# A soft-cap attention with a soft mixture of experts on one core: who takes four exponential tiles, and the order of the first and last stages

## The chip, the cores and the metric

The kernel runs on one NeuronCore of one Trainium2 chip. The metric is the device time of one execution in microseconds (us), the median over several runs. The engines are PE (matrix multiply; PEld are its weight loads), DVE (vector), ACT (activations), POOL and SP; SP, POOL and ACT also issue DMA transfers.

## The reference

```python
# q, k, v: 8 batches x 12 heads x 448 x 64; cap = 30; 8 experts, 4 slots each
scores = cap * tanh((q @ k.T / sqrt(64)) / cap)
attn = softmax(scores)                 # over the 448 keys
x = (attn @ v), heads joined           # 3584 x 768
logits = x @ phi                       # 3584 x 32
d = softmax(logits, axis=0); c = softmax(logits, axis=1)
slot_input = d.T @ x                   # 32 x 768, 4 rows per expert
slot_out[e] = relu(slot_input[e] @ w1[e]) @ w2[e]     # 768 -> 1024 -> 768
out = c @ slot_out                     # 3584 x 768, float32
```

The softmax over the rows of `logits` runs over all 3584 tokens.

## The kernel before

**Attention.** Two heads of four make a pair, and a pair's scores are seven tiles of 128 x 448. There are 48 pairs, so 336 tiles, laid in one order and cut into `NCH` = 56 chunks of six. A chunk j takes two score groups from PE (three tiles each, into one of two PSUM buffers `sc`), two tanh on ACT (L301, 1344 columns each) that write the tile `ex` of the chunk, and an exponential over the chunk in place (L305, `exp_chunk`), which is issued one chunk later. Five `ex` buffers rotate.

**Shared tiles.** In most chunks ACT's exponential leaves out the first tile (`exp_part(j, len(shared[j]), CH)`, 2240 columns in place of 2688). DVE computes that tile with five operations, numbered 0 to 4 in `poly_exp` (L332 to L337), on one scratch tile `work`. `PARTS` tells, for each j modulo 7 save 4, in which slot of which chunk each operation stands, and `EXTRA` does the same for chunks 3, 4, 5 and 50 to 53.

**Order of work.** The order is written out by hand: each chunk has slots ("a", "b", "c", "d" and some more), `at(j, slot, f)` puts a job into one, and `run(j, slot)` issues its jobs, those marked "<" first and those marked ">" last. Each engine works through its own instructions in that order and waits on semaphores for the others. Matmuls with V (`pv`, L355), the division by the row sum (L362, L365), transposes, logits, exponentials of logits and slot sums follow two chunks and more behind. `spare`, `fill` and `busy` issue matmuls on ones whose results nobody reads.

**Head.** `first_pieces` brings the first two heads into place: casts to bf16 on DVE and ACT, transposes on PE ("turn", L219) into PSUM tiles, copies back (L221). It works in two parts of q (tiles 0 to 3, 4 to 6) and of k (0 to 2, 3 to 6). The first score group (L292) needs all of q and the first part of k.

**End of attention.** After the last chunk (j = 55) its exponential is issued in three parts. Pairs 46 and 47 are multiplied in halves (`pvm`, `pvl`), then come the last logits, their exponential `E`, the last slot sums, and `e_norm`, which adds up the sums of `E` in `zacc` and, in the last batch, gives `rz`, the reciprocal that scales both experts' first layer. `clear_hpad` clears a padded tile for the hidden activations on POOL; it lies where `work` lay. `id32` is an identity in float32 for the last logits.

**Experts and output.** `layer1(i, half)` (L747) gives 512 of 1024 hidden columns of four experts at a time; `relu` reads them from PSUM; `h_transp` puts them into `hpad`. `layer2` (L780) goes through 64 blocks for the first 384 output columns, `so[0]` takes the result, then again for the other 384, `so[1]`. The output has 28 tiles of 128 x 768 (64 rows from each of two batches): `half_tile` makes one half of one tile with a matmul (L815), a multiply on ACT or DVE (L819, L817) and a store of 192 KB (`obh`). The first halves of the first ten tiles are put between the blocks of the second `layer2`; those of tiles 10 and 11 come after the copy of `so[1]`. Then the second halves of the first `NH` tiles follow, and the remaining tiles are made whole (L862, L869, L871) and stored two at a time (`ob`, 768 KB). SP issues every store (L796), and before that the loads of the second layer's weights, `w2t` (L729).

Of the kernel before, what the change touches and what calls it, by code (L numbers as in the profile page):

```python
# [10 lines left out]
BF16 = mybir.dt.bfloat16  # L11
I32 = mybir.dt.int32
U16 = mybir.dt.uint16
ALU = mybir.AluOpType
ACT = mybir.ActivationFunctionType
PSUM = bass.MemoryType.PSUM

P = 128
HP = 64
NT = 7  # L20
DH = 64
S = 448
CH = 6
CS = 3
# [12 lines left out]
def kernel(  # L37
# [12 lines left out]
    B, H, _, _ = q.shape  # L50
# [5 lines left out]
    HD = D // 2  # L56
    NFT = F // P
    cap = float(cap)
# [4 lines left out]
    NPAIR = 2 * NQ  # L63
# [145 lines left out]
    def first_pieces(h, jobs):  # L209

        for stage, nm, c0, c1, eng, bank, at0 in jobs:
            copy = act.copy if eng is act else dve.tensor_copy
            cols = slice(h * HP, h * HP + HP)
            if stage == "cast":
                copy(casts[nm, 0][:, c0:c1, cols],
                     raws[nm, 0][h][:, c0 * DH:c1 * DH].rearrange("p (c d) -> p c d", d=DH))
            elif stage == "turn":
                for c in range(c0, c1):
                    pe.transpose(bank[cols, at0 + c - c0, :], casts[nm, 0][:, c, cols], ident)  # L219
            else:  # L220
                copy(qkT[nm, 0][cols, c0:c1, :], bank[cols, at0:at0 + c1 - c0, :])  # L221

    def first_half(h):
        for nm in ("k", "q"):
            if h == 0:
                qkT[nm, 0] = qk.tile([P, NT, P], BF16, name=nm + "T", tag=nm + "T")
        one = psT.tile([P, 8, P], BF16, name="ps1", tag="T")
        two = psV.tile([P, NT, P], BF16, name="ps2", tag="pv")
        if h == 0:

            three = boots[1][:, CS - 1, :].bitcast(BF16).rearrange("p (c q) -> p c q", q=P)
            first_pieces(h, (("cast", "q", 4, NT, act, None, 0), ("cast", "k", 0, CS, dve, None, 0),
                             ("cast", "q", 0, 4, dve, None, 0), ("turn", "q", 4, NT, pe, three, 0),
                             ("turn", "k", 0, CS, pe, two, 0), ("copy", "q", 4, NT, act, three, 0),
                             ("turn", "q", 0, 4, pe, one, 0), ("copy", "k", 0, CS, dve, two, 0),
                             ("cast", "k", CS, NT, act, None, 0), ("copy", "q", 0, 4, dve, one, 0),
                             ("turn", "k", CS, NT, pe, three, 3), ("copy", "k", CS, NT, dve, three, 3)))
        else:
            first_pieces(h, (("cast", "k", 0, NT, dve, None, 0), ("cast", "q", 0, NT, dve, None, 0),
                             ("turn", "k", 0, NT, pe, two, 0), ("turn", "q", 0, NT, pe, one, 0),  # L240
                             ("copy", "k", 0, NT, dve, two, 0), ("copy", "q", 0, NT, dve, one, 0)))
            for nm in ("q", "k"):
                raws.pop((nm, 0)), casts.pop((nm, 0))
                load(nm, 2)
# [59 lines left out]
    def exp_part(j, u0, u1):  # L304
        act.activation(exs[j][:, u0:u1, :], exs[j][:, u0:u1, :], ACT.Exp, scale=cap)  # L305

    def exp_chunk(j):
        exp_part(j, len(shared.get(j, ())), CH)

# [8 lines left out]
    EXTRA = {3: (((0, "a", (0,)), (0, ">b", (1,)), (0, "<d", (2, 3)), (1, "a", (4,)),),), 4: (((0, "a", (0,)), (0, ">d", (1, 2)), (1, "<b", (3,)), (1, "r", (4,)),),), 5: (((0, ">b", (0,)), (0, "<d", (1,)), (0, ">d", (2, 3)), (1, "r", (4,)),),), 50: (((0, "<d", (0,)), (0, ">d", (1, 2, 3)), (1, "a", (4,)),),), 51: (((0, "<b", (0,)), (0, ">b", (1,)), (0, ">d", (2,)), (1, ">b", (3, 4)),),), 52: (((0, "c", (0, 1)), (0, "<d", (2,)), (0, ">d", (3, 4)),),), 53: (((0, "<b", (0,)), (1, "a", (1,)), (1, "<b", (2,)), (1, "<d", (3,)), (1, ">d", (4,)),),)}  # L318
    shared = {j: (PARTS[j % 7],) for j in range(6, NCH - 6) if j % 7 in PARTS}
    shared.update(EXTRA)  # L320
    if cap >= 50:
        shared = {}

    lead = POW2[0] / FRAC ** 3
    p2, p1, p0 = (c / POW2[0] * FRAC ** (n + 1) for n, c in enumerate(POW2[1:]))
    halves16 = xe.bitcast(U16).rearrange("p (s two) -> p s two", two=2)
    frac, whole = halves16[:, :, 0], halves16[:, :, 1]

    def poly_exp(j, u, ops):
        t = exs[j][:, u, :]  # L330
        steps = (
            lambda: dve.tensor_scalar(xe, t, cap * math.log2(math.e) * FRAC,  # L332
                                      (127 + math.log2(lead)) * FRAC, ALU.mult, ALU.add),
            lambda: dve.tensor_scalar(xb.bitcast(U16), whole, 7, None, ALU.logical_shift_left),  # L334
            lambda: dve.scalar_tensor_tensor(xp, frac, p2, frac, ALU.add, ALU.mult),  # L335
            lambda: dve.scalar_tensor_tensor(xp, xp, p1, frac, ALU.add, ALU.mult),  # L336
            lambda: dve.scalar_tensor_tensor(t, xp, p0, xb, ALU.add, ALU.mult))  # L337
        for n in ops:
            steps[n]()
# [175 lines left out]
    def at(j, slot, f, *a):  # L515
        if j < 0:
            j, slot = 0, "b"
        aux.setdefault((j, slot), []).append((f, a))

    def clear_hpad():  # L520

        hpads.append(consts.tile([P, E, NFT, NS], BF16, name="hpad", tag="work", bufs=1))
        pool.memset(hpads[0], 0.0)
# [19 lines left out]
    for b in range(B):  # L543
# [20 lines left out]
        if b < B - 1:  # L564
# [6 lines left out]
                at(*when("en"), e_norm, b)  # L571
            if b % 2:
                at(*when("es"), e_sums, b // 2)
    for j, tiles in shared.items():
        for u, parts in enumerate(tiles):
            for dj, slot, ops in parts:
                at(j + dj, slot, poly_exp, j, u, ops)
    for n, job in enumerate(wjobs):
        at(1 + n * (NCH - 5) // len(wjobs), "b", *job)
    for j, slot, n in ((0, "a", 10), (0, "c", 10), (1, "b", 10), (1, "c", 8)):  # L580
        at(j, slot, spare, n)
    for j, slot, n in ((NCH - 6, "d", 8), (NCH - 4, "d", 8), (NCH - 2, "d", 12)):
        at(j, slot, spare, n)
    at(0, "c", init_vbd, 0)
    at(1, "c", init_vbd, 1)
    at(0, "d", vcast, 0)

    def run(j, slot):
        for part in ("<", "", ">"):
            for f, a in aux.pop((j, part + slot), []):  # L590
                f(*a)
# [6 lines left out]
    def busy(n, home=None, by=None):  # L598
        by = ones if by is None else by
        for _ in range(n):  # L600
            pe.matmul(junk if home is None else home, by, by, start=True, stop=True)  # L601
# [13 lines left out]
    for j in range(NCH):  # L615
# [31 lines left out]
        run(j, "c")  # L647
        qk_chunk(2 * j + 3)
        run(j, "d")
    last = NPAIR - 1  # L650
    assert place[last, 0] == NTILE - NT and pair_at[NCH - 3] == last - 2
    CL = CS
    exp_part(NCH - 1, len(shared.get(NCH - 1, ())), CL)
    exp_part(NCH - 1, CL, CH - 1)
    exp_part(NCH - 1, CH - 1, CH)
    attp.close()
# [3 lines left out]
    def bank(shape, dt=F32, name="bank"):  # L660
        return big.tile(shape, dt, name=name, tag="b")
# [5 lines left out]
    pv2 = [bank([P, 4, W], name=f"pvl{half}") for half in range(2)]  # L667
    junk = bank([P, P], name="junk")
    xq_tile(last - 1)
    run(NCH - 1, "t0")  # L670
    for half, gs in enumerate(halves):
        pv_mms(last - 1, 0, NT, gs, pvm[half])
        norm(last - 1, cuts[half], cuts[half + 1], pvm[half])
        run(NCH - 1, f"t{half + 1}")
        if half == 0:
            logits(NQ - 2)
    for half, gs in enumerate(halves):
        pv_mms(last, 0, NT - CH + CL, gs, pv2[half])
    clear_hpad()
    assert not aux, aux.keys()  # L680
    hpad = hpads[0]
    x_transp(last - 1)
    for half, gs in enumerate(halves):
        pv_mms(last, NT - CH + CL, NT - 1, gs, pv2[half])
# [30 lines left out]
        js = slice(3 * s, 3 * s + 3)  # L715
        dve.tensor_tensor(slT[:, js, :], sl_ps[:, js, :], slacc[:, js, :], op=ALU.add)
    e_rep(bl)
    busy(4)
    e_norm(bl)
    att.close()  # L720


# [27 lines left out]
        return i, half, hp  # L750

    def relu(i, half, hp):
        f0, f1, mid = 512 * half, 512 * half + 512, 512
        if i == half == 1:
            mid = f0 + 288
        if f0 < mid:
            f2 = min(f1, mid)
            act.activation(hbs[i][:, f0:f2], hp[:, 0:f2 - f0], ACT.Relu, scale=rz)
        if mid < f1:
            f2 = max(f0, mid)  # L760
            dve.tensor_scalar(hbs[i][:, f2:f1], hp[:, f2 - f0:512], rz, 0.0, ALU.mult, ALU.max)

    def h_transp(i):

# [18 lines left out]
                      start=(n0 == 0), stop=(n0 == len(blocks) - 4))  # L783

    first = [layer1(0, half) for half in range(2)]
    for hp in first:
        relu(*hp)
    relu(*layer1(1, 0))
# [30 lines left out]
            act.mul(ob, home, winv[:, bb, c:c + 1])  # L819
        store(n, half, half + 1, ob)  # L820

    NH, NHL = 12, 10
    so = [wts.tile([P, HD], BF16, name=f"so{half}", tag="w1", bufs=E) for half in range(2)]
    n2 = len(blocks)
    for n0 in range(0, n2, 4):
        if n0 == n2 // 2 - 8:
            h_transp(1)
        layer2(n0, 0)
    HB = HD // 2
    act.copy(so[0][:, 0:HB], so_ps[0][:, 0:HB])  # L830
    dve.tensor_copy(so[0][:, HB:HD], so_ps[0][:, HB:HD])
    done = 0
    for n0 in range(0, n2, 4):
        layer2(n0, 1)

        if n0 % 8 == 4 and n0 != n2 // 2 + 4 and done < NHL:
            for eng in ("act", "dve") if n0 < n2 // 2 else ("act",):
                half_tile(done, 0, bank([P, HD], name="op0") if done else
                          [bank([P, HD // 2], name="op00") for _ in range(2)], eng)
                done += 1  # L840
    dve.tensor_copy(so[1], so_ps[1])
    for done in range(NHL, NH):
        half_tile(done, 0, bank([P, HD], name="op0"), "dve" if done % 2 else "act")
    mid.close()


# [64 lines left out]
```

## Time and profile before

| what | us |
|---|---|
| median of 3 runs (302.83 to 303.19) | 303.07 |
| the profiled execution's own time | 303.19 |
| its span in the profile | 301.4 |
| ACT busy in it | 267.8 (89%) |
| PE busy | 265.1 (88%) |
| DVE busy | 238.4 (79%) |
| POOL busy | 136.7 (45%) |

All times below count from the start of the span. A line of a group reads: source line, engine, operation, tile written and tiles read, partitions x elements and type, count; then busy time and mean ns of one; then idle time of the engine just before these instructions, and what ended most of it. In a timeline a row gives start, duration, engine, line and the number of neighbouring instructions merged. In the chain of work that ended last, a row's duration is its step in the chain.

### The profile page before, as it was taken

The page shows a single profiled execution, that of the slowest core. Times are in us where ns is not written, and L with a number is a line of the kernel's source. Part 1 is how long each engine was busy: PE and PEld are TensorE (multiplying, and loading weights), DVE is VectorE, ACT ScalarE, POOL GpSimd, SP SyncE. Part 2 cuts the span into 40 slices and gives each one's busy share as a digit, 9 for nine tenths or more (in the row PEclk, how much of TensorE's full clock was granted, in tenths as well). Part 3 has the DMA queues.
Part 4 walks back from the last instruction along what each step waited for, and adds up shares of the span by engine and source line. Part 5 has one row for each costly group of instructions (what it writes and reads, how often), then busy time and mean ns, then how long its engine had stood idle before and what let it go on. Part 6 is the DMA issues. An engine that isn't in the chain of part 4 may idle for free.

```text
span 301.4 us, 10670 instructions
## 1 busy us (share of the span) xinstructions
PE 265.1 (88%) x4686; PEld 182.5 (61%) x4686; DVE 238.4 (79%) x515; ACT 267.8 (89%) x211; POOL 136.7 (45%) x176
## 2 busy tenths in 40 slices
PE   8898989998899989988999899899999999998820
PEld 6665656665666666666666566666666677642410
DVE  3728989898998999899879998999899974336840
ACT  3999999999999999999999999999999998226730
POOL 4493563485439534953394439444933232000000
PEclk9999999999999999999999999999999999999995
DMA  7999999799999999999899999999999649939997
GB/s 255 212 204 204 207 219 196 143 212 206 232 178 199 194 232 212 208 203 232 150 161 219 230 225 181 197 230 232 171 197 231 199 118 338 369 127 350 381 413 318
DMA packets 57917, 67.70 MB, mean 225 GB/s; under 512 B 3856, under 2 KB 54160, under 8 KB 57872
## 3 DMA queue, kind: packets, MB, share of 16 engines
q0 software_dynamic: 42448, 35.31, 76.0%
q1 hardware_dynamic: 15136, 31.50, 29.6%
q8 instruction: 36, 0.59, 0.7%
q10 hardware_dynamic: 288, 0.23, 0.2%
q14 instruction: 9, 0.07, 0.1%
HBM read 91.32 MB, written 18.87 MB: 366 GB/s over the span
## 4 chain that ended last, share of the span: by engine, by line
ACT 69%; PE 18%; issue 4%; DVE 4%; POOL 1%; DVEq 0%; ACTq 0%
ACT ex L301 38%; ACT ex L305 28%; PE pv L355 3%; PE so_ps L780 2%; PE sc L292 2%; PE hp L747 2%; PE op L862 1%; ACT ob L871 1%; PE boot L601 1%; PE op L815 1%; ACT E L445 1%; DVE xq L365 1%; PE junk L601 1%; PE pvl L355 1%; DVE ob L869 1%
## 5 line engine op out<-in xcount | busy, mean ns | idle before, releaser
L301 ACT ACTIVATE ex<-sc 128x1344 bf16<-128x1344 f32 (+1 forms) x113 | 164.2, 1726 | 1.4 <-PE sc L292 1.4
L305 ACT ACTIVATE ex<-ex 128x2240 bf16<-128x2240 bf16 (+4 forms) x58 | 147.1, 2572 | 0.1
L355 PE MATMUL pv<-vbd,ex 128*128 128x130 bf16 (+1 forms) x1610 | 94.5, 211 | 10.3 <-POOL vbd L270 5.1
L355 PEld LDWEIGHTS <-ex 128*128 128x128 bf16 (+1 forms) x1680 | 75.9, 101 | 30.8 <-issue 6.6
L292 PE MATMUL sc<-qT,kT 64*64 64x448 bf16 x672 | 68.9, 359 | 4.2 <-ACT ex L301 3.2
L270 POOL CAST vbd<-vraw 64x896 bf16<-64x896 f32 x23 | 22.4, 974 | 65.6 <-PE pv L355 48.1
L451 POOL COPY e<-E 128x512 bf16<-128x512 bf16 x9 | 5.5, 616 | 64.6 <-ACT E L445 33.9
L336 DVE SCALAR_TENSOR_TENSOR work<-work 128x448 f32<-128x448 f32 x45 | 32.6, 725 | 0.8
L335 DVE SCALAR_TENSOR_TENSOR work<-work 128x448 f32<-128x448 uint16 x45 | 31.8, 706 | 0.0
L292 PEld LDWEIGHTS <-kT 64*64 64x64 bf16 x672 | 24.7, 105 | 10.6 <-issue 6.7
L337 DVE SCALAR_TENSOR_TENSOR ex<-work 128x448 bf16<-128x448 f32 x45 | 30.0, 667 | 0.7
L365 DVE TENSOR_TENSOR xq<-pv,rec 128x448 bf16<-128x448 f32 x46 | 28.7, 624 | 1.6
L271 POOL CAST vbd<-vraw 64x896 bf16<-64x896 f32 x23 | 24.3, 1057 | 1.4
L110 POOL DMA_DIRECT2D w1b<-in_moe_w_dram x32 | 24.6, 771 | 0.0
L414 DVE COPY xT<-xps 128x448 bf16<-128x448 bf16 x47 | 18.3, 389 | 7.4 <-PE xps L408 6.7
L601 PEld LDWEIGHTS <-ones 128*128 128x128 bf16 x315 | 19.3, 102 | 6.6 <-issue 4.3
L601 PE MATMUL junk<-ones 128*128 128x128 bf16 x279 | 20.4, 220 | 1.1 <-DVE xq L365 0.8
L332 DVE TENSOR_SCALAR work<-ex 128x448 int32<-128x448 bf16 x45 | 20.6, 458 | 0.0
L262 DVE COPY kT<-kps 128x896 bf16<-128x896 bf16 x23 | 14.3, 622 | 6.4 <-PE kps L260 6.0
L334 DVE TENSOR_SCALAR work<-work 128x448 uint16<-128x448 uint16 x45 | 18.7, 415 | 0.5
L182 POOL DMA_DIRECT2D kb<-in_k_dram x22 | 16.0, 729 | 5.5 <-PE kps L260 5.4
L182 POOL DMA_DIRECT2D qb<-in_q_dram x22 | 16.2, 736 | 3.6 <-DMA kraw<-in_k_dram 3.6
(122 smaller groups left out, 338.6 us busy)
## 6 DMA issues: line engine op xcount, KB each, us to landing
w1b<-in_moe_w_dram POOLq DMA_DIRECT2D x32, 384.0 KB, 8.5
vraw<-in_v_dram SPq DMA_DIRECT2D x23, 448.0 KB, 5.0
w2d<-in_moe_w_dram POOLq DMA_DIRECT2D x20, 384.0 KB, 8.9
w2t<-w2d SPq DMA_DIRECT2D x20, 384.0 KB, 6.0
out_dram<-ob SPq DMA_DIRECT2D x7, 768.0 KB, 6.9
qb<-in_q_dram POOLq DMA_DIRECT2D x22, 224.0 KB, 8.6
kb<-in_k_dram POOLq DMA_DIRECT2D x22, 224.0 KB, 7.8
w2b<-in_moe_w_dram POOLq DMA_DIRECT2D x12, 384.0 KB, 8.8
```

What stands on the lines that cost most here:

```text
L110: pool.dma_start(out=w1b[e][:, js, fs], in_=w1r[:, e, js, fs])
L182: (sp if nm == "v" else pool).dma_start(out=t, in_=quad_ap(nm, Q))
L271: pool.tensor_copy(t[HP:P, :, :, DH + 1:VW - 1], raw[HP:P])
L292: pe.matmul(sc[cs, u, 0:S], qkT["k", Q][r, c, cs], qkT["q", Q][r, :, cs], start=True, stop=True)
L301: act.activation(exs[j][:, half * CS + u0:half * CS + u1, :], sc[:, u0:u1, 0:S], ACT.Tanh, scale=qk_scale / cap)
L305: act.activation(exs[j][:, u0:u1, :], exs[j][:, u0:u1, :], ACT.Exp, scale=cap)
L335: lambda: dve.scalar_tensor_tensor(xp, frac, p2, frac, ALU.add, ALU.mult),
L336: lambda: dve.scalar_tensor_tensor(xp, xp, p1, frac, ALU.add, ALU.mult),
L337: lambda: dve.scalar_tensor_tensor(t, xp, p0, xb, ALU.add, ALU.mult))
L355: pe.matmul(out_, exs[j][r, u, q0:q0 + (HP if tail else P)], v_, start=(c == 0 and g == gs[0] < NF), stop=(c == NT - 1), skip_group_check= ...
L365: dve.tensor_tensor(xq[Q][:, h, s0:s1, :], pv[:, 0:s1 - s0, 0:DH], rec.to_broadcast([P, s1 - s0, DH]), op=ALU.mult)
L601: pe.matmul(junk if home is None else home, by, by, start=True, stop=True)
```

## The change

- The list `shared` is made anew: chunks from 6 to 53 whose j modulo 7 has an entry in `PARTS`. `EXTRA` goes. So chunks 3, 4, 5 and 53 (53 modulo 7 is 4) have no shared tile any more, and chunks 50, 51 and 52 take the places in `PARTS`.
- In the head the jobs of `first_pieces` stand in another order, and the third PSUM tile, borrowed from `boots[1]`, goes: q 4 to 6 is turned into the free part of `two`, k 3 to 6 into the free part of `one`.
- `clear_hpad` moves to the last chunk's slot "a", ahead of `id32`.
- `e_norm` of the last batch moves behind the first two `layer1` calls; in its old place `busy(4)` becomes `busy(8)`.
- `relu` of the last hidden quarter is one operation on DVE, not one on ACT and one on DVE.
- `so[0]` is copied whole by ACT, not half by ACT and half by DVE.
- `NH` is 10 in place of 12: tiles 10 and 11 are made whole, after the second halves of tiles 0 to 9.

```diff
-            three = boots[1][:, CS - 1, :].bitcast(BF16).rearrange("p (c q) -> p c q", q=P)
-            first_pieces(h, (("cast", "q", 4, NT, act, None, 0), ("cast", "k", 0, CS, dve, None, 0),
-                             ("cast", "q", 0, 4, dve, None, 0), ("turn", "q", 4, NT, pe, three, 0),
-                             ("turn", "k", 0, CS, pe, two, 0), ("copy", "q", 4, NT, act, three, 0),
-                             ("turn", "q", 0, 4, pe, one, 0), ("copy", "k", 0, CS, dve, two, 0),
-                             ("cast", "k", CS, NT, act, None, 0), ("copy", "q", 0, 4, dve, one, 0),
-                             ("turn", "k", CS, NT, pe, three, 3), ("copy", "k", CS, NT, dve, three, 3)))
+            first_pieces(h, (("cast", "k", 0, CS, dve, None, 0), ("cast", "q", 0, 4, dve, None, 0),
+                             ("cast", "q", 4, NT, act, None, 0), ("turn", "k", 0, CS, pe, two, 0),
+                             ("copy", "k", 0, CS, dve, two, 0), ("turn", "q", 0, 4, pe, one, 0),
+                             ("cast", "k", CS, NT, act, None, 0),
+                             ("copy", "q", 0, 4, dve, one, 0), ("turn", "q", 4, NT, pe, two, CS),
+                             ("copy", "q", 4, NT, act, two, CS),
+                             ("turn", "k", CS, NT, pe, one, 4), ("copy", "k", CS, NT, dve, one, 4)))
...
-        exp_part(j, len(shared.get(j, ())), CH)
+        exp_part(j, 1 if j in shared else 0, CH)
...
-    shared = {j: (PARTS[j % 7],) for j in range(6, NCH - 6) if j % 7 in PARTS}
-    shared.update(EXTRA)
+    shared = [j for j in range(NCH - 2) if j % 7 in PARTS and j > 5] if cap < 50 else []
...
+    at(NCH - 1, "a", clear_hpad)
...
-    clear_hpad()
...
     e_rep(bl)
-    busy(4)
-    e_norm(bl)
+    busy(8)
...
-        if i == half == 1:
-            mid = f0 + 288
...
+        if half == 0:
+            act.activation(hbs[i][:, 0:512], hp, ACT.Relu, scale=rz)
+        else:
+            dve.tensor_scalar(hbs[i][:, 512:1024], hp, rz, 0.0, ALU.mult, ALU.max)
...
     first = [layer1(0, half) for half in range(2)]
+    e_norm(B - 1)
     for hp in first:
         relu(*hp)
...
-    NH, NHL = 12, 10
+    NH = 10
...
-    act.copy(so[0][:, 0:HB], so_ps[0][:, 0:HB])
-    dve.tensor_copy(so[0][:, HB:HD], so_ps[0][:, HB:HD])
+    act.copy(so[0], so_ps[0])
...
     dve.tensor_copy(so[1], so_ps[1])
-    for done in range(NHL, NH):
-        half_tile(done, 0, bank([P, HD], name="op0"), "dve" if done % 2 else "act")
```

More of the change, by code (lines that the diff above doesn't have):

```diff
@@ L317 @@
              6: ((0, "<b", (0,)), (0, "c", (1, 2)), (0, "<d", (3,)), (1, "a", (4,)))}
-    EXTRA = {3: (((0, "a", (0,)), (0, ">b", (1,)), (0, "<d", (2, 3)), (1, "a", (4,)),),), 4: (((0, "a", (0,)), (0, ">d", (1, 2)), (1, "<b", (3,)), (1, "r", (4,)),),), 5: (((0, ">b", (0,)), (0, "<d", (1,)), (0, ">d", (2, 3)), (1, "r", (4,)),),), 50: (((0, "<d", (0,)), (0, ">d", (1, 2, 3)), (1, "a", (4,)),),), 51: (((0, "<b", (0,)), (0, ">b", (1,)), (0, ">d", (2,)), (1, ">b", (3, 4)),),), 52: (((0, "c", (0, 1)), (0, "<d", (2,)), (0, ">d", (3, 4)),),), 53: (((0, "<b", (0,)), (1, "a", (1,)), (1, "<b", (2,)), (1, "<d", (3,)), (1, ">d", (4,)),),)}
-    shared = {j: (PARTS[j % 7],) for j in range(6, NCH - 6) if j % 7 in PARTS}
-    shared.update(EXTRA)
-    if cap >= 50:
-        shared = {}
+    shared = [j for j in range(NCH - 2) if j % 7 in PARTS and j > 5] if cap < 50 else []
     lead = POW2[0] / FRAC ** 3
@@ L327, with poly_exp @@
     frac, whole = halves16[:, :, 0], halves16[:, :, 1]
-    def poly_exp(j, u, ops):
-        t = exs[j][:, u, :]
+    def poly_exp(j, ops):
+        t = exs[j][:, 0, :]
         steps = (
@@ L573 @@
                 at(*when("es"), e_sums, b // 2)
[L574 to L577, printed above, removed]
+    for j in shared:
+        for dj, slot, ops in PARTS[j % 7]:
+            at(j + dj, slot, poly_exp, j, ops)
     for n, job in enumerate(wjobs):
@@ L649 @@
         run(j, "d")
-    last = NPAIR - 1
+    assert not aux, aux.keys()
+    last, hpad = NPAIR - 1, hpads[0]
     assert place[last, 0] == NTILE - NT and pair_at[NCH - 3] == last - 2
     CL = CS
-    exp_part(NCH - 1, len(shared.get(NCH - 1, ())), CL)
+    exp_part(NCH - 1, 0, CL)
     exp_part(NCH - 1, CL, CH - 1)
@@ L669 @@
     xq_tile(last - 1)
-    run(NCH - 1, "t0")
     for half, gs in enumerate(halves):
@@ L673 @@
         norm(last - 1, cuts[half], cuts[half + 1], pvm[half])
-        run(NCH - 1, f"t{half + 1}")
         if half == 0:
@@ L678 @@
         pv_mms(last, 0, NT - CH + CL, gs, pv2[half])
-    clear_hpad()
-    assert not aux, aux.keys()
-    hpad = hpads[0]
     x_transp(last - 1)
@@ L752, in relu @@
     def relu(i, half, hp):
-        f0, f1, mid = 512 * half, 512 * half + 512, 512
-        if i == half == 1:
-            mid = f0 + 288
[L756 to L761, printed above, removed]
+        if half == 0:
+            act.activation(hbs[i][:, 0:512], hp, ACT.Relu, scale=rz)
+        else:
+            dve.tensor_scalar(hbs[i][:, 512:1024], hp, rz, 0.0, ALU.mult, ALU.max)
     def h_transp(i):
@@ L828 @@
         layer2(n0, 0)
-    HB = HD // 2
-    act.copy(so[0][:, 0:HB], so_ps[0][:, 0:HB])
-    dve.tensor_copy(so[0][:, HB:HD], so_ps[0][:, HB:HD])
+    act.copy(so[0], so_ps[0])
     done = 0
@@ L834 @@
         layer2(n0, 1)
-        if n0 % 8 == 4 and n0 != n2 // 2 + 4 and done < NHL:
+        if n0 % 8 == 4 and n0 != n2 // 2 + 4 and done < NH:
             for eng in ("act", "dve") if n0 < n2 // 2 else ("act",):
@@ L841 @@
     dve.tensor_copy(so[1], so_ps[1])
-    for done in range(NHL, NH):
-        half_tile(done, 0, bank([P, HD], name="op0"), "dve" if done % 2 else "act")
+    assert done == NH
     mid.close()
```

## The prediction

> **What bounds the kernel now.** I read the chain of work that ended last first, then the groups, then the chain in order of time, then the stretch around each edit. The chain's shares and the two scalar-engine groups:
>
> ```profile
> ACT 69%; PE 18%; issue 4%; DVE 4%; POOL 1%; DVEq 0%; ACTq 0%
> L301 ACT ACTIVATE ex<-sc 128x1344 bf16<-128x1344 f32 (+1 forms) x113 | 164.2, 1726 | 1.4 <-PE sc L292 1.4
> L305 ACT ACTIVATE ex<-ex 128x2240 bf16<-128x2240 bf16 (+4 forms) x58 | 147.1, 2572 | 0.1
> ```
>
> After the 1.4 us before the first tanh, ACT is idle for 0.1 us in both groups together. Its records overlap, so the price of one instruction is its step in the chain:
>
> ```profile
> 23.88 2.36 ACT ex L301 x2
> 26.24 1.96 ACT ex L305
> 28.20 2.36 ACT ex L301 x2
> 30.56 1.96 ACT ex L305
> ...
> 91.78 2.33 ACT ex L305
> ```
>
> Two tanh take 2.36 us, an exponential of five tiles (2240 columns) 1.96, one of six (2688, at 91.78) 2.33: a tile is worth 0.37 us of ACT. From 6.98 to about 244.6 us whatever ACT gets or loses moves the end. Then the chain leaves ACT:
>
> ```profile
> 246.66 0.68 PE sc L292 x6
> 247.35 0.79 PE junk L601 x12
> 248.18 0.84 PE pv L355 x12
> ...
> 253.17 0.85 PE pvm L355 x21
> 254.02 1.04 PE pvl L355 x20
> ```
>
> From 244.66 PE's own work runs end to end. The last stage is the stores', by the table of stretches (columns: stretch, then busy us of PE, PEld, DVE, ACT, POOL, granted clock, DMA share, GB/s):
>
> ```profile
> 269.00:271.00 2.00, 1.75 (x29) 0.63 (x17) 1.07 (x3) 0.74 (x2) 0.00 (x0) 1.00 0.04 8
> 277.00:279.00 2.00, 1.63 (x7) 0.55 (x7) 1.74 (x4) 1.66 (x4) 0.00 (x0) 1.00 1.04 367
> 289.00:291.00 2.00, 0.74 (x4) 0.21 (x3) 1.39 (x2) 0.90 (x1) 0.00 (x0) 1.00 1.03 424
> ```
>
> DMA is empty until the first store (270.77), then full to 299 while the engines stop at 291: the end is the first store plus bytes over rate, plus any gap in the stream. Half stores (192 KB) go at 367 GB/s, 196.6 KB / 367 = 0.536 us each; the 768 KB ones, by the DMA view of 284 to 290, at 416, 1.89 us each.
>
> The profiled execution took 303.19 us with a span of 301.4, 0.12 over the median of 303.07; I add the sum to the median.
>
> **Part 1, the shares.** The new `shared` list drops chunks 3, 4, 5 and 53 (53 mod 7 is 4, which has no entry). DVE loses 4 x 5 operations, by their groups' means 0.46 + 0.42 + 0.71 + 0.73 + 0.67 = 2.97 us a tile; ACT gets 4 exponentials of 2688 in place of 2240. Chunks 50 to 52 keep their share with other places on DVE, hidden as in every batch: nothing. For chunks 3 to 5: 3 x 0.373 = **+1.12 us** (1.10 to 1.14). DVE's relief returns nothing, since ACT waits there for nobody.
>
> Chunk 53 is computed after PE took over, so only what exceeds PE's slack counts. Its exponential ends at 244.74 + 3.01 = 247.75, and the pv matmuls that need it start at 248.18; with 0.37 more it ends at 248.12, and weight load and start put them at about 248.27, 0.09 late. The exponential of chunk 54 ends at 251.26, needed 251.88: covered. The first part of the last one:
>
> ```profile
> 251.37 2.27 ACT L305 ACTIVATE ex<-ex 128x1344 bf16<-128x1344 bf16 x1
> 253.95 0.23 PE L355 MATMUL pvl<-vbd,ex 128*128 128x130 bf16 x1
> ```
>
> By the timeline of PE and ACT (all single starts here are from it) it ends at 253.65, 0.3 before its reader; plus 0.37 it is 254.02, and the reader starts at about 254.17. The two later parts end at 254.49 and 254.95 and are read at 255.41 and 256.04: covered. So **+0.2** (0 to 0.37).
>
> **Part 2, the first tiles.** The old order gave three tiles of PSUM to the four groups of transposes; the new one packs them into two, and the built program's waits show what follows: the turn of q 4..7 (into `two`) waits for DVE's copy of k, the turn of k 3..7 (into `one`) for DVE's copy of q 0..4. The old rows:
>
> ```profile
> 4.60 0.95 PE L219 MATMUL ps<-ident,casts 128*64 128x128 bf16 x7
> 4.84 0.47 ACT L221 COPY qT<-boot 64x384 bf16<-64x384 bf16 x1 [0.71 <-PE boot L219]
> 5.16 0.35 DVE L221 COPY kT<-ps 64x384 bf16<-64x384 bf16 x1 [0.65 <-PE ps L219]
> 5.59 0.42 DVE L221 COPY qT<-ps 64x512 bf16<-64x512 bf16 x1
> 6.19 1.41 PE L292 MATMUL sc<-qT,kT 64*64 64x448 bf16 x12
> ```
>
> Seven transposes in 0.95 us, the last 0.31 long, are 0.107 apart. New: k is cast by 4.31 as before, its turn starts at 4.37 and ends 4.90; copy k 4.94 to 5.28; turn q 4..7 from 5.33, ends 5.86; ACT copies it 5.90 to 6.37; scores at 6.42 instead of 6.19. Everything behind ACT's first tanh moves: **+0.23** (0.1 to 0.3). The other copies and the second scores (old 6.84, new about 7.0) still come before ACT's third tanh part at 8.2.
>
> PE's transposes at 8.09 (14 in 0.94 us) are 0.055 apart, so PE ran at half pace until about 6.0, whatever the granted clock of 1.00 says. The new order puts two waits of about 0.2 us in that stretch. If the pace rises only after the scores, their 0.75 us doubles: +0.55 on top, which I take for a rival. The Trainium skill, "TensorE: Matmul & The Clock Gate", Part 1, says that full rate follows a window of about 3.4 us of sustained activity which runs free of the kernel's start; that speaks against new gaps here, and by it alone the 0.55 would come or not by chance.
>
> **Part 3, end of attention and both expert layers.** `clear_hpad` goes ahead of the `id32` cast on POOL: 1.80 us, now from about 244.2, after DVE's last step of chunk 52; behind it on POOL stand id32, there by 246.4 and needed at 256.7, and an E copy of 259.25; SP's w2t loads wait for the vbd cast ahead of it: nothing. `e_norm(B-1)` moves behind 48 layer1 matmuls, with four more fillers in its old place, so layer1 still starts at 260.26 with slT. Its four matmuls (260.00 to 260.33 in the old trace) now stand on PE's path, and both relus wait for rz: sums 263.35, zacc 0.16, reciprocal 0.16 and handoffs give 263.8 instead of 263.06, and h_transp(0), old 264.26, waits for the DVE relu (0.75) until about 264.55. **+0.27** (0.2 to 0.35). The undivided relu, 0.75 on DVE, replaces 0.50 on ACT and then 0.45 on DVE (266.08 to 267.06): from 266.37 to 267.12, just when PE gets there: nothing.
>
> The copy of so[0] was split, but its halves ran one after the other:
>
> ```profile
> 269.25 0.32 ACT L830 CAST so<-so_ps 128x192 bf16<-128x192 f32 x1 [2.67 <-PE so_ps L780]
> 269.60 0.36 DVE L831 CAST so<-so_ps 128x192 bf16<-128x192 f32 x1 [1.94 <-ACT so L830]
> ```
>
> One ACT copy of 384 columns is not in the trace. Between the 192 columns at 0.32 and the multiply of 384 at 0.58 I take 0.48. The end comes 0.71 - 0.48 = 0.23 sooner, but the first product, which needed only ACT's half, starts later, so the first store gains **-0.14** (-0.25 to 0).
>
> **Part 4, NH from 12 to 10.** Four half stores become one pair of whole tiles: 1.89 - 4 x 0.536 = **-0.25** (to 0), DMA time. But tiles 10 and 11 fed the stream while so[1] was copied:
>
> ```profile
> 275.26 0.56 DVE L841 CAST so<-so_ps 128x384 bf16<-128x384 f32 x1 [1.57 <-PE so_ps L780]
> 275.87 0.34 PE L815 MATMUL op<-so,ET 128*128 128x384 bf16 x1 [0.24 <-DVE so L841]
> ...
> 276.12 0.33 SPq L796 DMA_DIRECT2D out_dram<-obh  x1
> ```
>
> The 11th store was issued at 276.12 and landed 1.9 us later, 0.53 after the tenth (277.49). Without it the 11th is tile 0's second half: so[1] done 275.82, product to 276.21, DVE's multiply of 0.62 to 276.87, issue 276.90, landing 278.80 instead of 278.02. **+0.78** of empty DMA. Half stores took 1.9 to 2.5 us from issue to landing: with 2.5 for this one the gap is 1.4, with 2.5 for the tenth (2.1) it is 0.4; I keep 0.4 to 1.4 and take the 1.9, since this store, like the old 11th, meets an empty queue. SP then issues every 0.5 us against 0.536 of moving, so no second gap. The Trainium skill, "DMA: Bandwidth & Descriptors", Anatomy of one DMA, gives about 2.0 us plus bytes / 436e3 per DMA, 2.45 here; by that the gap would be 1.3.
>
> **Sum:** 1.12 + 0.20 + 0.23 + 0.27 - 0.14 - 0.25 + 0.78 = 2.21; 303.07 + 2.21 = **305.3 us**.
>
> **Rivals.** *Half pace in the head*: +0.55, 305.8. For: the pace turned only 0.2 us before the scores. Against: PE is busier than idle there. Chance 0.13. *No gap in the stores*: the ten half stores are still moving when the next arrives; without the 0.78, 304.5. For: the stream has a small backlog by then. Against: the 11th store landed after the bare 1.9 us, so there was none. 0.15. *Not slower*: the small stores run at the big ones' rate once SP has fewer of them to issue. Then 20 x (0.536 - 0.473) = 1.26 goes, and with no gap either the sum is 2.21 - 1.26 - 0.78 = 0.17, 303.2. It decides if half stores land less than 0.49 us apart; against it, the DMA share is already 1.03 to 1.04 there. 0.04; a gain over that needs ACT to shorten, which nothing removed does. *Not what it says*: the words tell of a moved tile, but the built program shows four shares gone (six-tile exponentials 10 to 14); that is in the sum. The forecast itself has 0.63; 0.05 is for costs unseen.
>
> **Numbers.** All low ends give 1.3, all high ends with the half pace near 4; 8 in 10 lie between 304.0 and 306.4. A measurement tells 0.2%, 0.6 us, from no change: faster 0.03, same 0.04, slower 0.93.
>
> **What would show it.** Right: scores at 6.4; four more steps of 2.33 with no ACT gap; PE unbroken from about 246.0; a first store about 1.7 later; a landing gap of 1.3 instead of 0.53 after the tenth. Wrong: ACT idle between 8 and 240; half stores closer than 0.49; scores spread over 1.5 us.

## Result and the profile after

| | median us | range us | runs |
|---|---|---|---|
| before, same chip | 302.95 | 302.79 to 303.19 | 4 |
| changed kernel | 305.47 | 305.23 to 305.99 | 4 |

The ratio is 1.0085 (95% interval 1.0067 to 1.0102): 2.5 us slower, against 2.2 forecast. A few executions in the longer series below take 2 to 3 us more and stay in the ratios, so a ratio there need not be that of the two medians. The profiled execution took 305.99 us with a span of 303.3. Line numbers after the change are lower by some (L355 is L351, L365 is L361, L601 is L597, L747 is L738, L780 is L766, L815 is L802, L830 is L816, L841 is L826).

The page: shares of the chain that ended last, and the two scalar-engine groups.

```profile
ACT 58%; PE 20%; DVE 9%; issue 4%; DMA 4%; POOL 2%; DVEq 0%; ACTq 0%; POOLq 0%
L301 ACT ACTIVATE ex<-sc 128x1344 bf16<-128x1344 f32 (+1 forms) x113 | 164.6, 1732 | 0.8 <-PE sc L292 0.8
L305 ACT ACTIVATE ex<-ex 128x2240 bf16<-128x2240 bf16 (+4 forms) x58 | 148.9, 2603 | 0.1
```

ACT is again idle for 0.1 us in both groups together once it has started. The share of ACT in the chain fell from 69% to 58% because the chain now often jumps from ACT to an engine that is just in time for it and back; ACT's own rows have no gap. In the chain in order of time (start, step, what):

```profile
23.56 2.36 ACT ex L301 x2
25.93 2.33 ACT ex L305
28.26 2.36 ACT ex L301 x2
30.62 2.33 ACT ex L305
32.95 2.36 ACT ex L301 x2
35.31 2.33 ACT ex L305
```

These are the exponentials of chunks 3, 4 and 5, now six tiles each: 2.33 where the rows of before have 1.96. Later in the same chain:

```profile
248.24 0.79 PE junk L597 x12
249.07 0.84 PE pv L351 x12
...
254.06 0.85 PE pvm L351 x21
254.91 1.05 PE pvl L351 x20
...
260.74 0.55 PE junk L597 x8
261.30 2.70 PE hp L738 x48
264.00 0.27 PE zps L455 x4
264.27 1.41 PE hp L738 x24
265.67 0.29 PE hps L755 x8
```

Up to `pvl` the steps are as long as before and only start 0.89 later. New in it are eight fillers instead of four, and the four `zps` matmuls of `e_norm` behind `hp`.

The same milestones in three profiles. The last is a second profiled execution of the changed kernel (a1_after below), whose head ran at the same pace of PE as that of before:

| start, us | before | after | after, second | rise in after | rise in second |
|---|---|---|---|---|---|
| first tanh | 6.98 | 6.66 | 7.22 | -0.32 | +0.24 |
| first `pvl` matmul | 253.95 | 254.84 | 255.31 | +1.21 | +1.12 |
| first `hp` matmul | 260.26 | 261.23 | 261.69 | +0.08 | +0.07 |
| first `hps` (`h_transp(0)`) | 264.26 | 265.61 | 266.07 | +0.38 | +0.38 |
| copy of `so[0]` | 269.25 | 270.56 | 271.02 | -0.04 | -0.04 |
| first store issued | 270.77 | 271.93 | 272.39 | -0.15 | -0.15 |
| 10th store landed | 277.49 | 278.62 | 279.08 | -0.03 | -0.03 |
| 11th store landed | 278.02 | 279.92 | 280.37 | +0.77 | +0.76 |
| last store landed | 300.27 | 301.93 | 302.38 | -0.24 | -0.24 |
| end of span | 301.42 | 303.27 | 303.70 | +0.19 | +0.17 |
| sum | | | | +1.85 | +2.28 |

A rise is the change of the distance to the row above it. Below the head the two executions agree within 0.1 in every row. The time outside the span was 1.8 us in before and in the second (305.47 us in all), but 2.7 in the first execution; no row of the trace tells why.

### The profile page after: what moved, and what is told of

It reads as the page before. It is cut to its first block, busy times and chain, and to the rows that moved or that the text cites. A ratio compares the mean times of both kernels' runs of the same rounds, so it can differ in the third digit from the quotient of the medians.

```text
span 303.3 us, 10644 instructions
## 1 busy us (share of the span) xinstructions
PE 263.9 (87%) x4690; PEld 182.1 (60%) x4690; DVE 227.8 (75%) x493; ACT 269.0 (89%) x209; POOL 137.0 (45%) x176
## 4 chain that ended last, share of the span: by engine, by line
ACT 58%; PE 20%; DVE 9%; issue 4%; DMA 4%; POOL 2%; DVEq 0%; ACTq 0%; POOLq 0%
ACT ex L301 31%; ACT ex L305 24%; PE pv L351 5%; DMA qb<-in_q_dram 3%; PE sc L292 2%; PE so_ps L766 2%; PE hp L738 2%; DVE xq L361 2%; PE op L846 2%; ACT ob L855 1%; DVE work L332 1%; PE op L802 1%; PE junk L597 1%; DMA kraw<-in_k_dram 1%; DVE work L331 1%
## 5 line engine op out<-in xcount | busy, mean ns | idle before, releaser
L305 ACT ACTIVATE ex<-ex 128x2240 bf16<-128x2240 bf16 (+4 forms) x58 | 148.9, 2603 | 0.1
L351 PE MATMUL pv<-vbd,ex 128*128 128x130 bf16 (+1 forms) x1610 | 94.4, 211 | 10.3 <-DVE xq L361 5.3
L351 PEld LDWEIGHTS <-ex 128*128 128x128 bf16 (+1 forms) x1680 | 75.9, 101 | 30.8 <-issue 6.6
L332 DVE SCALAR_TENSOR_TENSOR work<-work 128x448 f32<-128x448 f32 x41 | 30.3, 738 | 0.7
L361 DVE TENSOR_TENSOR xq<-pv,rec 128x448 bf16<-128x448 f32 x46 | 28.7, 625 | 1.6
L331 DVE SCALAR_TENSOR_TENSOR work<-work 128x448 f32<-128x448 uint16 x41 | 28.1, 686 | 0.0
L333 DVE SCALAR_TENSOR_TENSOR ex<-work 128x448 bf16<-128x448 f32 x41 | 26.5, 647 | 0.6
L597 PEld LDWEIGHTS <-ones 128*128 128x128 bf16 x319 | 19.2, 101 | 6.2 <-issue 4.3
L597 PE MATMUL junk<-ones 128*128 128x128 bf16 x283 | 20.6, 220 | 0.8 <-DVE xq L361 0.3
L328 DVE TENSOR_SCALAR work<-ex 128x448 int32<-128x448 bf16 x41 | 19.2, 468 | 0.3 <-ACT ex L301 0.3
L358 DVE RECIPROCAL rec<-pv 128x7 f32<-128x7 f32 x46 | 9.4, 204 | 12.1 <-PE pv L351 11.8
```

The lines of the kernel that those rows point to most:

```text
L351: pe.matmul(out_, exs[j][r, u, q0:q0 + (HP if tail else P)], v_, start=(c == 0 and g == gs[0] < NF), stop=(c == NT - 1), skip_group_check= ...
L361: dve.tensor_tensor(xq[Q][:, h, s0:s1, :], pv[:, 0:s1 - s0, 0:DH], rec.to_broadcast([P, s1 - s0, DH]), op=ALU.mult)
```

## The experiments

All are edits of the kernel before, except a1_after, which is the changed kernel. Medians are compared with the kernel before on the same chip.

**e1_head: the new order of the first tiles alone.**

```diff
-            first_pieces(h, (("cast", "q", 4, NT, act, None, 0), ("cast", "k", 0, CS, dve, None, 0),
+            first_pieces(h, (("cast", "k", 0, CS, dve, None, 0), ("cast", "q", 0, 4, dve, None, 0),
...
```

> The kernel before with the head's new order alone. The prediction's step says that the two waits on DVE's copies put the first scores 0.23 us later: 303.2 us, ratio 1.0008. The trace of the change says otherwise: its scores came 2.09 us after the first cast of k started, against 2.23 before (cast at 3.78 and 3.96), with transposes 0.055 us apart where they were 0.107. Theory A, the order itself gains: scores 2.1 us after the cast, 0.15 less time, ratio 0.9995. Theory B, PE's pace at that moment differs from one execution to the next and the order does nothing to it: transposes 0.107 apart here, scores about 2.45 us after the cast, ratio 1.0008 or, with executions of both kinds, 1.000.

303.24 against 303.16, ratio 1.0005 (0.9997 to 1.0014). By this measurement alone the new order costs nothing that can be told from zero. The reason is in the heads of the executions. That of after, by the timeline (start, us, engine, line, operation, then the idle time before it and its releaser):

```profile
3.78 0.35 DVE L215 CAST casts<-kraw 128x192 bf16<-128x192 f32 x1 [2.78 <-DMA kraw<-in_k_dram]
4.19 0.61 PE L219 MATMUL ps<-ident,casts 128*64 128x128 bf16 x7 [0.20 <-DVE casts L215]
4.99 0.72 PE L219 MATMUL ps<-ident,casts 128*64 128x128 bf16 x7 [0.18 <-DVE kT L221]
5.35 0.47 ACT L221 COPY qT<-ps 64x384 bf16<-64x384 bf16 x1 [0.26 <-PE ps L219]
5.87 1.32 PE L292 MATMUL sc<-qT,kT 64*64 64x448 bf16 x12 [0.17 <-ACT qT L221]
```

Seven transposes took 0.61 us, not 0.95, and are mostly 0.056 apart: PE was already at full pace. The releasers are those forecast: q 4..7 behind DVE's copy of k, the scores behind ACT's copy of q. The scores then come 2.09 after the cast of k. In the kernel before they come 2.23 after it at half pace, but 1.80 at full pace, as in e2_shares, which has the old head:

```profile
4.41 0.60 PE L219 MATMUL ps<-ident,casts 128*64 128x128 bf16 x7
5.79 1.41 PE L292 MATMUL sc<-qT,kT 64*64 64x448 bf16 x12
```

with its cast at 3.99. Five executions of the old order at full pace have 1.79 to 1.98, three at half pace 2.23 to 2.29, and one whose pace turned among these transposes (e3_enorm) 2.01; of the new order three at full pace have 2.09 (e1_head, after and e11_rest), one at half pace 2.42. So at equal pace the new order costs 0.1 to 0.3, and the pace, which changes from one execution to the next, moves the scores by 0.25 to 0.5.

**e2_shares: the shares of chunks 3, 4, 5 and 53 dropped, all else as before.**

```diff
     shared.update(EXTRA)
+    for j in (3, 4, 5, 53):
+        shared.pop(j)
```

> The kernel before without the shared tiles of chunks 3, 4, 5 and 53, nothing else changed (the places of chunks 50 to 52 stay). The prediction: 3 x 0.373 for chunks 3 to 5 and 0.2 for chunk 53, in all +1.32 us, 304.3, ratio 1.0044. The rival from the trace of the change, where PE's pv matmuls after chunk 53 shifted no more than those before: chunk 53 costs nothing, +1.12, ratio 1.0037. If DVE's relief gave anything back it would be under 1.0.

304.31 against 303.16, ratio 1.0044 (1.0029 to 1.0059), +1.15. From the first tanh to the first `pvl` the trace has 248.09 instead of 246.97: +1.12, the three steps of 0.373. The interval of the times holds both forecasts, with a price for chunk 53 (1.0044) and without (1.0037); the trace is for the second.

**e5_share53: only chunk 53's share dropped** (the loop above over `(53,)`).

> The kernel before without the shared tile of chunk 53 alone. The prediction: +0.2 us (0 to 0.37), ratio 1.0007, with the first pv matmul after that exponential about 0.1 late and the first pvl matmuls another 0.1. The rival, from the trace of the change: PE owns this stretch and ACT's 0.37 us stay inside its slack, so the first store comes no later against the first scores than in the kernel before: ratio 1.000, and at most 0.06 us at the second weight load of pvl.

303.04 against 303.05, ratio 0.9989 (0.9964 to 1.0014). The trace is finer: from the first tanh to the first `pvl` 247.06, the same as in e3_enorm and e6_so_relu (247.05), which keep that share. Behind it there are 0.02: the first `hp` comes 6.32 after the first `pvl` in this run and in e2_shares, 6.30 in before. (The 247.06 and 247.05 are 0.08 to 0.09 over the 246.97 of before. The difference grows evenly, 0.03 by 98 us after the first tanh, 0.05 by 138 and 0.08 by 217; some executions have it and others not, whatever their edit, and why stays open.)

**e3_enorm: `e_norm` behind the first `layer1` calls, four more fillers; e8_enorm_busy4: the same without the fillers.**

```diff
-    busy(4)
-    e_norm(bl)
+    busy(8)          # busy(4) in e8_enorm_busy4
...
     first = [layer1(0, half) for half in range(2)]
+    e_norm(B - 1)
```

> The kernel before with the last e_norm behind the first two layer1 calls and busy(8) in its old place, nothing else. The prediction: +0.27 us, 303.2, ratio 1.0009. By the trace of the change it is more: layer1 started 0.06 late behind the fillers, and h_transp(0) came 0.38 later still, since both relus waited for rz: +0.44, 303.4, ratio 1.0015. A rival that the stores hide it gives 1.000.

> The kernel before with the last e_norm behind the first two layer1 calls, but busy(4) kept: the move without the four more fillers. If the fillers delayed layer1, it now starts 0.06 us sooner against the last slot sums than in the kernel with busy(8); h_transp(0) should still come 4.38 us after the first layer1 matmul, in place of 4.00, if the wait of both relus for rz is the cost, and 4.1 if only the four matmuls are.

e3_enorm: 303.68 against 303.16, ratio 1.0024 (1.0001 to 1.0047). From the first `hp` to the first `hps` it takes 4.38 us in both, as in after, against 4.00. Without the added fillers `hp` comes 3.87 after the last `pvl`, before 3.94, with them 4.00: the fillers cost 0.13, not nothing, since `slT` is there early enough for layer1 to gain a little without them. First tanh to first store: 263.79 before, 264.11 in e8_enorm_busy4 (a single execution, 303.43 us), 264.31 in e3_enorm, 264.22 without the even growth of 0.09 told of above, which e3_enorm has and e8_enorm_busy4 has not. The expectation of e8_enorm_busy4 took 4.38 for the sign that the wait for `rz` is the cost, and 4.1 for the four matmuls. The 4.38 came, but it does not decide this: the four matmuls alone make it, as the rows under `e_norm` below show.

**e4_nh10 and e10_nh8: the number of tiles with half stores.**

```diff
-    NH, NHL = 12, 10
+    NH = NHL = 10     # 8 in e10_nh8
```

> The kernel before with NH = NHL = 10, so that tiles 10 and 11 are made whole later, nothing else. The prediction: a gap of 0.78 us in the stores after the tenth, less 0.25 for larger stores: +0.53, 303.5, ratio 1.0017; the 11th store lands 1.3 us after the tenth, in place of 0.53. The rival (no gap, smaller stores saved): -0.25, ratio 0.9992.

> The kernel before with NH = NHL = 8: only eight first halves are there to feed the stores before so[1] is copied. The gap theory: without two more products PE ends layer2 about 0.35 us sooner, the ninth store lands near 278.45 on the old clock in place of 276.97, so the gap is 1.5 us instead of none (NH = 10: 0.78), and eight half stores become two pairs, -0.5: +1.0 us, ratio 1.0033. If what NH = 10 costs has another cause than a stream without work (packets, SP), NH = 8 should not cost more than NH = 10 by that amount: ratio 1.0015 or less.

e4_nh10: 303.77 against 303.16, ratio 1.0027 (1.0014 to 1.0040), +0.61. The 11th store lands 1.31 us after the 10th instead of 0.53, the stream ends 0.49 later behind the first store, and the span's end comes 1.32 after the last landing instead of 1.15: +0.66 in the trace. e10_nh8: 303.69 against 303.05, ratio 1.0010 (0.9991 to 1.0029). Its hole is between the 8th and 9th store, 1.60 apart. By the table of stretches (columns as in the prediction) of e10_nh8:

```profile
276.00:278.00 2.00, 1.43 (x7) 0.50 (x6) 1.74 (x4) 1.64 (x3) 0.00 (x0) 1.00 0.48 171
278.00:280.00 2.00, 1.98 (x12) 1.01 (x12) 1.42 (x3) 1.98 (x3) 0.27 (x1) 1.00 1.04 368
```

DMA is half empty (0.48) in the one and full in the other. The hole grew by 1.07, not by the 1.5 that my +1.0 rested on, because the second `layer2`, with two half tiles fewer between its blocks, ended sooner (`so[1]` is copied 3.72 us after the first store's issue, before 4.49). Behind the first store the stream ends 0.57 later, and the end of the span comes 1.02 after the last landing: +0.44 in the trace. By the times alone the expectation's mark went the other way: it gave a ratio of 1.0015 or less to the rival of another cause (packets, SP), and 1.0010 came, with medians 0.64 apart. What speaks for the hole is the trace, in which "hole minus cheaper stores" is 1.07 - 0.5 = 0.57, as measured; the +1.0 was too large for this kernel.

**e6_so_relu and e12_so_relu_again: the copy of `so[0]` and the last relu undivided** (the same edit in both).

```diff
-    act.copy(so[0][:, 0:HB], so_ps[0][:, 0:HB])
-    dve.tensor_copy(so[0][:, HB:HD], so_ps[0][:, HB:HD])
+    act.copy(so[0], so_ps[0])
...
-            mid = f0 + 288
+            mid = f0
```

> The kernel before with so[0] copied whole by ACT and the last relu whole on DVE, nothing else: the two parts of the change that should gain. The prediction: -0.14 us and nothing, the trace of the change -0.15 and -0.04, so 302.9 to 303.0, ratio 0.9994; ACT's copy takes 0.48 in place of 0.71 for the two. The rival: two engines halve the work, so undoing the split costs about 0.2, ratio 1.0006.

> The kernel before with so[0] copied whole by ACT and the last relu whole on DVE, once more, since its interval reached 1.000: by its trace the first store comes 0.18 us sooner, ratio 0.9994; if the first result was noise, 1.000 or above.

302.78 against 303.05, ratio 0.9977 (0.9955 to 1.0000), and 302.95 against 303.16, ratio 0.9997 (0.9976 to 1.0018). The timeline of e6_so_relu:

```profile
268.97 0.48 ACT L830 CAST so<-so_ps 128x384 bf16<-128x384 f32 x1 [4.15 <-PE so_ps L780]
```

From this start to the first store's issue it takes 1.37 us, before 1.52. The trace's gain is 0.15 for the copy and about 0.04 for the relu; both medians point that way (0.27 and 0.21 lower), but the second interval contains no change, so it is not shown to be faster than the kernel before.

**a1_after and e11_rest: the whole change again, and all of it but the shares** (e11_rest also leaves `clear_hpad` in its old place).

> The changed kernel itself, timed in five rounds. The parts timed alone gave medians of +0.08 (head), +1.15 (shares), +0.52 (e_norm and fillers), +0.61 (NH = 10) and -0.27 (so[0] and last relu) against the kernel before: +2.1 if they add, ratio 1.0069. The prediction's own sum was 2.21, ratio 1.0073. If the parts hinder one another it is above 1.0085.

> All of the change except the shares: the new head, e_norm behind layer1, the whole last relu, so[0] whole on ACT and NH = 10, with the shared tiles of chunks 3, 4, 5 and 53 kept. By the prediction's terms 0.23 + 0.27 - 0.14 - 0.25 + 0.78 = 0.89, ratio 1.0029; by the parts timed alone 0.08 + 0.52 + 0.61 - 0.27 = 0.94, 1.0031. The rival, that ACT's four tiles explain all of the loss, gives 1.000 to 1.001.

a1_after: 305.68 against 303.16, ratio 1.0089 (1.0075 to 1.0103). This is above the 1.0085 that was named as the sign of parts that hinder one another, but the interval reaches to both sides of it. Its head, at half pace:

```profile
4.01 0.35 DVE L215 CAST casts<-kraw 128x192 bf16<-128x192 f32 x1 [3.01 <-DMA kraw<-in_k_dram]
4.42 2.04 PE L219 MATMUL ps<-ident,casts 128*64 128x128 bf16 x14
5.91 0.47 ACT L221 COPY qT<-ps 64x384 bf16<-64x384 bf16 x1 [0.57 <-PE ps L219]
6.43 1.32 PE L292 MATMUL sc<-qT,kT 64*64 64x448 bf16 x12
```

Scores at 6.43, where the prediction had 6.42: this is the execution that the prediction had described. e11_rest: 304.36 against 303.16, ratio 1.0042 (1.0029 to 1.0056), +1.20. The rival that ACT's four tiles explain all of the loss (1.000 to 1.001 here) is excluded. The 0.44% of e2_shares and the 0.42% here add up to 0.86%, the change has 0.89%: the shares are half of the loss, and no coupling of the two halves shows within the intervals. The medians of the single parts (0.08 + 1.15 + 0.52 + 0.61 - 0.27 or - 0.21) add up to 2.1 or 2.15 against the change's 2.52; the intervals are wider than this difference.

In e11_rest the first `pvl` came 247.42 after the first tanh, 0.37 more than in e3_enorm, although ACT's part is not touched. The view of PE's waits from 150 to 190 us (line waited for, releaser: us in total, times, longest):

```profile
PE qps L260 <- DMA qb<-in_q_dram: 1.2, 1, 1.2
```

A q load that POOL issued at 153.82 landed 9.14 us later, and PE stood still for it. In before the load with the same place landed after 7.94 us, and PE did not wait. A shorter delay was absorbed: in e1_head PE is 0.35 late at this transpose and on time at the one 30 us later. The move of `clear_hpad`, forecast at nothing, was not run alone; in after it runs on POOL from 245.40 to 247.20 with `id32` behind it until 247.56, and no row of the table has a rise that would be its own.

## Why the prediction was right

**Chunks 3 to 5: 1.12 forecast, 1.12 measured** in e2_shares and in the second execution (1.21 in the first, which has the even growth of 0.09). The step read from the chain, 2.33 less 1.96, was the price, while the busy time of the group (148.9 against 147.1 us) would have made 0.45 of each of the four tiles. DVE's relief (238.4 to 227.5 us busy in e2_shares, 12 forecast) returned nothing, as forecast.

**Chunk 53: 0.20 forecast, 0.02 measured.** The first half of this step was too tight: I charged 0.15 us from the exponential's end to its reader. In after the exponential ends at 249.01 and the reader starts at 249.07, 0.06 later and just when the fillers ahead of it end, so the slack of 0.43 covered the whole 0.37. The second half took the wrong reader. The first `pvl` matmul starts at 254.84 while the first part of the last exponential ends at 254.92, so it reads an older chunk (the first tile of pair 47 lies in chunk 54). What does wait is a later weight load of `pvl`: in the executions without this share it starts 0.12 behind the first `pvl` matmul, with it 0.07, and this is where the 0.02 come from. A shown start after a shown end is no proof of a dependence.

**Head: 0.23 forecast; 0.24 between executions at half pace, 0.1 to 0.3 at equal pace, -0.32 in the first pair.** The mechanism and the two new waits were right. What the step took for given was the pace of before's execution, which is not a property of the kernel. The Trainium skill, "TensorE: Matmul & The Clock Gate", Part 1 (the section on the HAM clock gate), says that the window runs free of the kernel, so that the turn varies between runs of the same program; the turns here agree with that, and so the first pair says little about the order. The rival of half pace in the head occurs in the kernel before too: in e10_nh8 and e12_so_relu_again, with the old order, the first tanh comes 1.05 and 1.03 after the scores' start instead of 0.79. There the pace turned among the scores (the first pairs start 0.38 and 0.28 apart, the later ones 0.19), which cost 0.25. A turn behind all of them, the case priced at 0.55, is in none of the thirteen profiles, and the change is not needed for either.

**`e_norm` and fillers: 0.27 forecast, 0.45 measured** (0.07 + 0.38 of the table). The rows of after:

```profile
263.93 0.33 PE L455 MATMUL zps<-ones,e 128*128 128x1 bf16 x4
264.20 1.48 PE L738 MATMUL hp<-w1b,slT 128*32 128x512 bf16 x24
264.50 0.16 DVE L461 RECIPROCAL rz<-zacc 128x1 f32<-128x1 f32 x1
264.70 0.75 DVE L747 TENSOR_SCALAR hb<-hp,rz 128x512 bf16<-128x512 f32 x1
264.74 0.69 ACT L745 ACTIVATE hb<-hp,rz 128x512 bf16<-128x512 f32 x1 [4.64 <-DVE rz L461]
265.61 0.36 PE L755 MATMUL hps<-ident,hb 128*128 128x16 bf16 x8
```

And of before, first from its chain, then from its timeline:

```profile
260.33 4.00 PE hp L747 x72
```

```profile
263.11 0.75 DVE L761 TENSOR_SCALAR hb<-hp,rz 128x512 bf16<-128x512 f32 x1 [2.39 <-PE hp L747]
264.26 0.36 PE L769 MATMUL hps<-ident,hb 128*128 128x16 bf16 x8
```

The waits came in the order forecast, and `rz` is even sooner: it ends 3.43 after the first `hp`, where I had 3.54. But they are not what moved the transposes. PE has no gap here: in the chains the 72 `hp` matmuls take 4.00 us in before, and in after 48 of them take 2.70, the four `zps` 0.27 and the other 24 take 1.41, 4.38 in all, with `hps` directly behind. So the 0.38 is the price of the four `zps` matmuls in PE's own queue, 0.27 for themselves and 0.11 for the change to them and back. The prediction had seen them on PE's path, gave them no price, and went by the wait of both relus for `rz`. That path is there and is shorter: the relus end at 265.43 and 265.45, and where PE does wait for DVE it starts 0.05 behind it (277.03 after the copy of `so[1]`, in the rows further below), so by the relus alone the transposes could have started at about 265.50, 4.27 behind the first `hp`, which is the 0.27 forecast. In before the relus were 0.40 ahead of PE (263.86 against 264.26). No run separates the two paths; this rests on the rows. The other 0.07 is `hp` itself, which does not start with `slT` as before, but behind the fillers; this too was taken for nothing.

**Last relu: nothing forecast, -0.04. Copy of `so[0]`: -0.14 forecast, -0.15.** The copy took 0.479 us, the estimate was 0.48.

**NH: +0.78 and -0.25 forecast, +0.77 and -0.24 measured**, and +0.17 to 0.19 behind the last landing, which was not in the sum. The hole in the stores is seen in the timeline and the table of stretches of after:

```profile
276.42 0.56 DVE L826 CAST so<-so_ps 128x384 bf16<-128x384 f32 x1 [1.58 <-PE so_ps L766]
277.03 0.66 PE L802 MATMUL op<-so,ET 128*128 128x384 bf16 x3 [0.67 <-DVE so L826]
277.41 1.14 DVE L804 TENSOR_SCALAR obh<-op,winv 128x384 f32<-128x384 f32 x2 [0.43 <-PE op L802]
```

```profile
276.50:278.50 2.00, 1.08 (x5) 0.50 (x6) 1.57 (x3) 0.69 (x3) 0.00 (x0) 1.00 0.86 303
278.50:279.50 1.00, 0.82 (x4) 0.29 (x3) 0.74 (x3) 1.00 (x2) 0.00 (x0) 1.00 0.62 220
279.50:281.50 2.00, 1.82 (x11) 0.85 (x10) 1.42 (x3) 1.67 (x4) 0.00 (x0) 1.00 1.04 367
289.00:291.00 2.00, 1.29 (x8) 0.51 (x6) 0.76 (x2) 0.92 (x2) 0.00 (x0) 1.00 1.03 424
```

Copy, product, multiply and issue stand one behind the other while DMA runs dry: against the 1.04 of the full stretch the first two lack 0.36 and 0.42 us of transfer, 0.78 together. The store issued at 278.05 landed at 279.92, after 1.87 us, the value taken. The estimate of 2.45 from the Trainium skill, "DMA: Bandwidth & Descriptors", Anatomy of one DMA, would have made the hole 1.3. That section gives its fit for DMAs of the software (gpsimd) path, while these stores go by SP, whose queue the profile lists as hardware_dynamic; the row decides for 0.77. The tail of 0.17 is in every profile with 30 stores (1.32 to 1.34 from last landing to end), and not in those with 33 (1.14 to 1.15) or 27 (1.02); what in the closing waits makes it was not tried.

**The rivals.** No gap in the stores: false, by the 1.30 between two landings. Half stores closer than 0.49: false, save at the hole they land 0.50 to 0.59 apart in every run, 0.54 in the mean. Of the signs named, scores at 6.4 and a first store 1.7 later failed in the first pair (5.87, and 1.16 later) and came in the second execution (6.43, and 1.62 later). The words of the change tell of a moved tile; what it costs comes from four shares that are gone, of which three matter, and from the parts at the end.

That the sum came out so near is in part luck: 0.18 too much in chunk 53 stood against 0.18 too little in `e_norm`, where the wrong path was priced, and 0.17 missing for the tail. The forecast of 2.21 stands beside 2.28 of span between the two executions at equal pace.

## What to carry to other kernels

Price a moved operation by the step it makes in the chain of its engine, not by its row's duration, and ask of each step only what exceeds the slack of the reader that the program names. Where two paths end at one instruction, price both: here a few matmuls in PE's own queue outweighed the wait that was drawn. A small store that fills a dry transfer queue while a copy is under way is worth more than the bytes that a larger store saves. Compare single executions only after the parts that vary between executions (here the head and one load) have been set side by side.

## What the hardware showed that was not expected

- PE's matmuls of 128 columns went from 0.107 to 0.056 us apart at a time that differs between executions, under fillers that begin at 0.78 in each: at 3.4 us after the start in after and e8_enorm_busy4, between 3.8 and 4.5 in six others, at 4.8 in e3_enorm, between 6.0 and 6.4 in before and a1_after, and among the scores, at about 6.8, in e10_nh8 and e12_so_relu_again. The granted clock of before, after and a1_after reads 1.00 from 0.5 to 7 us, so the pace has to be read from the spacing. The spread of 3.4 us is about the window that the Trainium skill, "TensorE: Matmul & The Clock Gate", Part 1, names; the 0.5 us either way that it gives for the turn is exceeded here.
- One q load in the middle of the kernel, behind weight loads in the same queue, took 7.7 to 9.1 us to land, though it was issued at the same point of ACT's chain. PE waited for it not at all in before, 0.2 us in after, 0.5 in e4_nh10 and e12_so_relu_again and 1.2 in e11_rest, where 0.37 us were left at the end of attention. In e12_so_relu_again nothing was left. e4_nh10 lost 0.2 there against e3_enorm, but with the same wait as e12_so_relu_again this is not shown to come from the load: in e4_nh10 PE also stood 0.95 and 1.00 us for DVE's addition of slot sums (`slacc`), at 183 and 214 us, and why stays open.
